# A long convolution and a gated FFN on one core: two filter spectra summed by accumulating transfers, one signal transform split by four, and a new instruction order

## The chip, the cores and the metric

The kernel runs on 1 core of one Trainium2 chip. The metric is device time in microseconds (us) of one execution. The profile comes from one execution, recorded by the hardware profiler.

## What is computed

With S = 2048 positions, D = 640 channels and F = 1728 hidden columns, all in bfloat16:

```
k_shift[t] = sum over u = 0..3 of k[t-u] * shift_k[:, u]
kv  = k_shift * v
y   = causal convolution of kv with ssm_k (length 2048) + kv * ssm_D
h   = x + layernorm(x) * y                 # x is A_q
out = h + (silu(n @ w_gate) * (n @ w_up)) @ w_down,   n = layernorm(h)
```

The reference writes the convolution as an FFT of length 4096. B_x is not used.

## The kernel before

**Blocks.** The sequence is cut into four blocks of 512 positions, i = 0..3, with 128 partitions and four positions to a partition. The filter is cut in the same way, m = 0..3. A block of 512 is taken to 256 complex frequencies by matmuls with a cosine and sine table (`ftab`). A spectrum is a tile of 128 partitions x [4 groups of frequencies][real, imaginary][640], 10,240 bytes on a partition. The output of block i needs the products of the signal spectrum X of block j with the filter spectrum C of block i-j, for all j up to i.

**Transforms.** `halves` (L573) does one in eight PSUM tiles, each of four matmuls of 320 columns (L582): the sums over even and over odd positions, for two groups of frequencies, cosine and sine. ACT evicts each tile (L595). `bfly` (L550, the add at L552) then makes the four groups out of the even and odd halves: four DVE adds or subtractions of 1280 elements for a spectrum. A second way, `quarters` (L613) with `spread` (L635), is in the source and is used by no block: eight tiles of two matmuls each, one position in four to a tile, and eight DVE operations of 1280 elements, of which six come ahead of the first product. A list, `R4` at L463, chooses between them.

**Filter spectra.** The filter is transformed in `kfwd` (L598). C0 and the raw spectra of pieces 1, 2 and 3 are made; R1 is the raw one of piece 1. `kcomb` (L660) then sums neighbours: C1 = R1 + C0, C3 = C3 + C2, C2 = C2 + R1, each as two DVE adds of 2560 elements (L666). C3 has to be summed before C2 is overwritten. For pieces listed in `KD` (L463, empty) it would issue an accumulating transfer from POOL's queue instead (L662), one for each spectrum, and the second would wait for the first.

**Products.** `prod(j, i)` (L743) multiplies X of block j with C of piece i-j for two halves of the frequencies: L753 and L754 multiply 2560 elements each, L759 adds twice 1280, and L769 adds the result into Y. The first product that uses C2 is prod(0, 2), the first that uses C3 is prod(0, 3).

**The rest of a block.** `kv` (L671) loads kT by a transposing transfer (L484 is the helper for those), runs the short convolution on PE (L691, L686), and multiplies by v on DVE; for blocks 1 to 3 the result goes back through transposing transfers into kvo, then L724 multiplies. `ln1` (L778) is the first layernorm: statistics on ACT (L791, L794; block 0 on DVE, L784), a power on POOL (L804), and L813 on ACT. `inverse` (L817) is the transform back (L830), from the tiles IE and IO, evicted by L854 and multiplied with x by L857 (block 0: L845), then the second layernorm with the statistics L868 and L870, the power on POOL (L881) and L886 (block 0: L889); four transposing transfers lay the result down as hnT. `ffn` (L896) is the FFN: 130 matmuls of 512 columns (L911, L912) and five more (L922), silu and a copy by ACT (L934, L936), a product on DVE (L938), and 104 matmuls down (L954), with 8 of half height (L966). ACT evicts their sums (L974) and DVE adds the residual (L981; block 3 does both in L984). SP stores the result (L988).

**What shares bytes.** IO lies on the bytes of kT, IE on those of hnT. X of block 1 lies on bytes of transforms of the filter, X of block 2 on those of R1, and X of block 3 on those of X of block 0. FO, the odd half of a signal transform, lies on kvo.

**Order.** Every operation is a task of a graph with its dependencies (`_Graph.add`, L98). `ORDER` (L307) lists the tasks of each engine, PE, ACT, DVE, POOL and SP, by number in the order of issue. `schedule` (L146) follows these lists and gives out the four PSUM units; its costs and due times only settle which unit a tile gets and how many filler matmuls (L249) PE runs in a long gap. `emit` (L230) writes the instructions with their semaphore waits. Each engine issues strictly in order, so an instruction that waits holds up all that stand behind it on its engine. Nearly all transfers are issued by SP (plain loads by the helper at L479).

Of the kernel before, what the change touches and what calls it, by code (L numbers as in the profile page):

```python
# [58 lines left out]
class _Graph:  # L59
# [170 lines left out]
    def emit(self, block):  # L230
# [75 lines left out]

ORDER = {  # L307
    "pe": """
# [6 lines left out]
    """,  # L315
    "act": """
# [12 lines left out]
    """,  # L329
    "dve": """  # L330
# [10 lines left out]
    """,  # L341
    "pool": """
        5 10 6 8 7 9 11 153 197 218 204 200 211 221 207 214 338 423 405 396 414 531 626 608 599 617 734 838 820 829 811
    """,
    "sp": """
# [3 lines left out]
    """,  # L349
}  # L350

# [1 line left out]
def bass_sequential_preLN__ssm_conv_h3__swiglu_ffn__prompt_kernel(  # L353
# [38 lines left out]
    with ExitStack() as es:  # L392
# [67 lines left out]
        epc = sb("epc", o + 544, [4], f32)  # L460
        assert o + 576 <= SBB + 16481 - A0, o + 576

        BN, DIRECT, D8, PT, BN2, ST, R4, PAIR, WARM, ACC, EA, KD, RD, LA, RA = (0,), (), (), (0,), (), (0,), (), True, 24, (), True, (), (), (1, 2, 3), (0, 1, 2)  # L463
        g = _Graph(nc, es)

        def cpe(n, k):
# [601 lines left out]
```

## Time and profile before

| what | value |
|---|---|
| median of 3 runs | 273.35 us (273.2 to 273.37) |
| span of the profiled execution | 269.5 us; the page gives no other time of that execution |
| granted PE clock, mean | 0.998 |
| filter transforms, PE L582 from KT | 128 matmuls, 299 or 300 ns each as shown |
| signal transforms, PE L582 from vt | 128 matmuls |
| DVE adds of filter spectra, L666 | 6, of 1480 to 1484 ns |
| DVE adds of signal transforms, L552 on X | 16, 818 ns each |
| first FFN matmul of blocks 0, 2, 3 | at 54.44, 168.53 and 222.09 us |

Times are in us from the start of the span. A row of a timeline gives the start, the length, the engine and line, the operation, output and inputs, the count, and in brackets the idle time of the engine ahead of it with what ended it. Matmuls are pipelined, so the mean of one, 300 ns, is longer than the step from one to the next. A row of the groups gives count, busy us and mean ns, and the idle time ahead.

### The profile page before, as it was taken

Reading aid. Unit: us, or ns where it says so; the run is one execution under the profiler, and the core shown is the slowest. Engines: PE = TensorE matmul, PEld = TensorE weight load, DVE = VectorE, ACT = ScalarE, POOL = GpSimd, SP = SyncE. Lnnn points to the kernel's source line nnn. Section 1 sums busy time; section 2 is a strip of 40 time slices with the busy share of each in tenths; the row PEclk is TensorE's granted clock in tenths of the full one; section 3 lists DMA queues with packets and bytes.
Section 4 is the critical chain, followed back from the end, with each engine's and each line's share of the span. In section 5 each row is a group of like instructions: output and inputs, shape, how many; then the busy total and the mean of one; then the engine's idle time right before and its main releaser. Section 6 shows DMA issues by size and latency. Waiting matters only on the chain.

```text
span 269.5 us, 4198 instructions
## 1 busy us (share of the span) xinstructions
PE 255.2 (95%) x1643; PEld 144.2 (53%) x1660; DVE 203.8 (76%) x282; ACT 206.9 (77%) x394; POOL 24.1 (9%) x35
## 2 busy tenths in 40 slices
PE   7799797999999999999999997999999999999995
PEld 5576455545444666554446574454446674444663
DVE  2399999899999999999999998999996100042312
ACT  2799999797889999479969997399889963647400
POOL 0000315000030013000200141000200200000000
PEclk9999999999999999999999999999999999999999
DMA  6999909551173608643000336510000050010002
GB/s 124 373 355 369 340 19 124 112 138 73 30 261 122 103 0 103 135 155 100 0 1 16 86 63 119 129 80 1 2 0 0 2 122 0 2 49 0 0 27 99
DMA packets 42501, 25.85 MB, mean 96 GB/s; under 512 B 32241, under 2 KB 41202, under 8 KB 42482
## 3 DMA queue, kind: packets, MB, share of 16 engines
q1 hardware_dynamic: 41824, 25.58, 35.7%
q8 instruction: 13, 0.21, 0.3%
q10 hardware_dynamic: 658, 0.01, 0.1%
q14 instruction: 6, 0.05, 0.1%
HBM read 15.69 MB, written 2.62 MB: 68 GB/s over the span
## 4 chain that ended last, share of the span: by engine, by line
DVE 41%; PE 27%; ACT 19%; DMA 6%; SPq 3%; issue 2%; POOL 1%; DVEq 0%
PE ps L954 11%; DVE T L753 6%; DVE T L754 6%; PE ps L912 6%; PE ps L911 5%; DVE T L759 5%; DVE Y L769 5%; DVE gu L938 4%; DVE X L552 3%; SPq L484 3%; DMA kT<-in_A_k_dram 3%; ACT KT L543 3%; ACT KO L595 2%; DVE C L666 2%; DMA kc<-in_A_ssm_k_dram 2%
## 5 line engine op out<-in xcount | busy, mean ns | idle before, releaser
L954 PE MATMUL ps<-Wd,gu 128*128 128x384 bf16 (+1 forms) x416 | 59.0, 299 | 0.2 <-ACT qo L854 0.2
L912 PE MATMUL ps<-hnT,UA 128*128 128x512 bf16 x140 | 53.1, 379 | 0.5
L911 PE MATMUL ps<-hnT,GA 128*128 128x512 bf16 x132 | 50.0, 379 | 1.3 <-DMA hnT<-qo 1.3
L954 PEld LDWEIGHTS ps<-Wd,gu 128*128 128x128 bf16 x416 | 40.0, 98 | 18.3 <-issue 1.3
L936 ACT ACTIVATE ub<-ps 128x512 bf16<-128x512 f32 (+1 forms) x60 | 33.7, 568 | 18.5 <-PE ps L912 11.3
L912 PE MATMUL ps<-hnT,UB 128*128 128x512 bf16 x120 | 45.5, 379 | 0.2
L911 PE MATMUL ps<-hnT,GB 128*128 128x512 bf16 x117 | 44.3, 379 | 0.0
L938 DVE TENSOR_TENSOR gu<-gu,ub 128x512 bf16<-128x512 bf16 x52 | 21.5, 421 | 25.1 <-ACT ub L936 13.2
L934 ACT ACTIVATE gu<-ps 128x512 bf16<-128x512 f32 x52 | 29.8, 596 | 12.6 <-PE ps L912 12.4
L753 DVE TENSOR_TENSOR T<-X,C 128x2560 bf16<-128x2560 bf16 x20 | 29.7, 1486 | 0.2
L754 DVE TENSOR_TENSOR T<-X,C 128x2560 bf16<-128x2560 bf16 x20 | 29.7, 1486 | 0.1
L911 PEld LDWEIGHTS ps<-hnT,GA 128*128 128x128 bf16 x140 | 13.7, 98 | 18.2 <-DMA hnT<-qo 1.9
L582 PE MATMUL ps<-KT,ftab 128*128 128x320 bf16 x128 | 19.9, 300 | 2.5 <-ACT KT L543 1.8
L912 PEld LDWEIGHTS ps<-hnT,UA 128*128 128x128 bf16 x140 | 13.7, 98 | 15.7
L881 POOL TENSOR_TENSOR mv<-mv,half 128x1 f32<-128x1 f32 x16 | 13.7, 859 | 68.2 <-ACT mv L874 68.2
L911 PEld LDWEIGHTS ps<-hnT,GB 128*128 128x128 bf16 x120 | 11.7, 98 | 14.2 <-ACT ub L936 0.2
L759 DVE TENSOR_TENSOR T<-T 128x1280 bf16<-128x1280 bf16 x24 | 19.2, 819 | 0.1
L912 PEld LDWEIGHTS ps<-hnT,UB 128*128 128x128 bf16 x120 | 11.7, 98 | 14.0
L582 PE MATMUL ps<-vt,ftab 128*128 128x320 bf16 x128 | 19.0, 299 | 0.1
L804 POOL TENSOR_TENSOR st<-st,half 128x8 f32<-128x8 f32 x4 | 7.9, 1981 | 113.1 <-ACT st L798 113.1
L769 DVE TENSOR_TENSOR Y<-Y,T 128x2560 bf16<-128x2560 bf16 x12 | 17.8, 1484 | 0.0
L582 PEld LDWEIGHTS ps<-KT,ftab 128*128 128x128 bf16 x128 | 11.0, 98 | 10.7 <-ACT KT L543 3.1
(86 smaller groups left out, 376.5 us busy)
## 6 DMA issues: line engine op xcount, KB each, us to landing
kc<-in_A_ssm_k_dram SPq DMA_DIRECT2D x4, 640.0 KB, 10.1
vt<-in_A_v_dram SPq DMA_DIRECT2D x4, 640.0 KB, 4.8
xh<-in_A_q_dram SPq DMA_DIRECT2D x4, 640.0 KB, 5.9
out_dram<-xh SPq DMA_DIRECT2D x16, 160.0 KB, 2.0
Wd<-in_B_w_down_dram SPq DMA_DIRECT2D x1, 1280.0 KB, 7.5
UA<-in_B_w_up_dram SPq DMA_DIRECT2D x1, 1120.0 KB, 13.5
GA<-in_B_w_gate_dram SPq DMA_DIRECT2D x1, 1120.0 KB, 10.5
UB<-in_B_w_up_dram SPq DMA_DIRECT2D x1, 960.0 KB, 7.5
```

What stands on the lines that cost most here:

```text
L582: last = e.matmul(pt.f(c, W), ftab[:, cs, j, f * P:(f + 1) * P], src[:, j, c * W:(c + 1) * W], start=(j == par), stop=(j == par + 2))
L753: g.add("dve", nm, lambda e, x=x, k=k, t1=t1: e.tensor_tensor(out=t1, in0=x, in1=k, op=ALU.mult), cdve(2560), r=[x, k], w=[t1])
L754: g.add("dve", nm, lambda e, x=x, k=ksw, t2=t2: e.tensor_tensor(out=t2, in0=x, in1=k, op=ALU.mult), cdve(2560), r=[x, k], w=[t2])
L759: g.add("dve", nm, lambda e, p=p, q=q, d=d, op=op: e.tensor_tensor(out=d, in0=p, in1=q, op=op), cdve(1280), r=[p, q], w=[d])
L769: g.add("dve", nm, lambda e, y=y, z=z: e.tensor_tensor(out=y, in0=y, in1=z, op=ALU.add), cdve(2560), r=[y, z], w=[y])
L881: g.add("pool", nm, lambda e, m=m: e.tensor_tensor(out=m[:, 3:4], in0=m[:, 2:3], in1=half[:, 1, 0:1], op=ALU.pow), 650, r=[m[:, 2:3], half ...
L911: e.matmul(pt.f(0, N), wg[:, c, f0:f0 + P], hnT[:, c, :], start=(c == 0), stop=(c == NC5 - 1))
L912: last = e.matmul(pt.f(1, N), wu[:, c, f0:f0 + P], hnT[:, c, :], start=(c == 0), stop=(c == NC5 - 1))
L934: g.add("act", nm, lambda e, pt=pt, gv=gv, a=ps_g, ts=ts: e.activation(out=gv, in_=pt.f(a[0], N, a[1])[:, ts], func=ACTF.Silu, scale=gain) ...
L936: g.add("act", nm, lambda e, pt=pt, uv=uv, a=ps_u, ts=ts: e.activation(out=uv, in_=pt.f(a[0], N, a[1])[:, ts], func=ACTF.Copy, scale=gain) ...
L938: g.add("dve", nm, lambda e, uv=uv, gv=gv: e.tensor_tensor(out=gv, in0=gv, in1=uv, op=ALU.mult), cdve(n), r=[gv, uv], w=[gv])
L954: last = e.matmul(pt.flat(c1 - c0, P + c0), slots[fb][:, j * P:(j + 1) * P], Wd[:, fb, c0:c1], start=(fb == 0 and not second), stop=(fb == ...
```

## The change

Three things change. `R4` names `xf2`, so the signal transform of block 2 goes through `quarters` and `spread`. `KD` names 2 and 3, so the sums for C3 and C2 are two accumulating transfers on POOL's queue (L662) and their four DVE adds go; C1 is summed by DVE still. And the lists of `ORDER` are all new.

```
-        BN, ..., R4, PAIR, WARM, ACC, EA, KD, RD, LA, RA = (0,), (), (), (0,), (), (0,), (), True, 24, (), True, (), (), (1, 2, 3), (0, 1, 2)
+        BN, ..., R4, PAIR, WARM, ACC, EA, KD, RD, LA, RA = (0,), (), (), (0,), (), (0,), ('xf2',), True, 24, (), True, (2, 3), (), (1, 2, 3), (0, 1, 2)

 "sp", its beginning, by what the numbers stand for:
-  ident, kT0, kc0, v0, ftab, x0, itab, kc1, UA, PK, kc3, kc2, x1, v1, Wd, UB, PK, GA, Wd, kT1
+  kc0, ident, kT0, x0, ftab, v0, kc2, PK, kc1, kc3, UA, GB, GA, itab, x1, v1, Wd, kT1, PK, Wd, UB
 "sp", the transposing transfers of block 1's hnT and block 2's kvo:
-  hnT, kvo, kvo, hnT, hnT, hnT, kvo, out, kvo, kvo
+  kvo, v2, kvo, kvo, kvo, hnT, kvo, hnT, out, hnT, hnT
 "pool":
-  ... L881 x4 (block 0), L804 (block 1), L881 x4 (block 1) ...
+  ... L881 x4 (block 0), C3 += C2, L804 (block 1), C2 += R1, L881 x4 (block 1) ...
 "pe", ahead of the FFN of block 0:
-  inverse of block 0 as IE, IO, IO, IE
+  inverse of block 0 as IO, IO, IE, IE
 "pe", around the FFN of block 1:
-  30 FFN matmuls, 32 of block 2's transform, 100 FFN matmuls
+  12 of block 2's transform, 10 FFN matmuls, 4 of the transform, 100 FFN matmuls, the five of L922, 20 FFN matmuls
```

In the new order DVE runs the butterflies of C2 and C3 together, ahead of the products of block 0's FFN, and in the new order the first product with C2 stands ahead of the L857 products of block 1, which were partly ahead of it. The inverse of block 1 is also split in another way over the matmuls down of block 0.

More of the change, by code (lines that the diff above doesn't have):

```diff
@@ L308 @@
     "pe": """
[6 rows of a table removed]
[7 rows of a table added]
     """,
     "act": """
[12 rows of a table removed]
[12 rows of a table added]
     """,
     "dve": """
[10 rows of a table removed]
[10 rows of a table added]
     """,
     "pool": """
-        5 10 6 8 7 9 11 153 197 218 204 200 211 221 207 214 338 423 405 396 414 531 626 608 599 617 734 838 820 829 811
+        5 6 10 11 8 7 9 151 202 195 209 205 216 198 212 219 134 336 135 421 403 394 412 529 610 628 601 619 736 822 813 840
+        831
     """,
     "sp": """
[3 rows of a table removed]
[3 rows of a table added]
     """,
@@ L461, in bass_sequential_preLN__ssm_conv_h3__swiglu_ffn__prompt_kernel @@
         assert o + 576 <= SBB + 16481 - A0, o + 576
-        BN, DIRECT, D8, PT, BN2, ST, R4, PAIR, WARM, ACC, EA, KD, RD, LA, RA = (0,), (), (), (0,), (), (0,), (), True, 24, (), True, (), (), (1, 2, 3), (0, 1, 2)
+        BN, DIRECT, D8, PT, BN2, ST, R4, PAIR, WARM, ACC, EA, KD, RD, LA, RA = (0,), (), (), (0,), (), (0,), ('xf2',), True, 24, (), True, (2, 3), (), (1, 2, 3), (0, 1, 2)
         g = _Graph(nc, es)
```

63 rows, old and new, of the table ORDER are left out of this document.

## The prediction

> **What bounds the kernel now.** I read the page's busy times, the table of windows, the chain of waits, and then timelines of PE, DVE, SP and POOL around each place that the diff moves.
>
> ```profile
> span 269.5 us, 4198 instructions
> PE 255.2 (95%) x1643; PEld 144.2 (53%) x1660; DVE 203.8 (76%) x282; ACT 206.9 (77%) x394; POOL 24.1 (9%) x35
> DVE 41%; PE 27%; ACT 19%; DMA 6%; SPq 3%; issue 2%; POOL 1%; DVEq 0%
> ...
> 13.00:54.40 41.40, 36.47 (x311) 23.55 (x313) 39.43 (x60) 39.38 (x65) 6.53 (x9) 1.00 0.80 220
> 54.40:110.00 55.60, 55.34 (x344) 30.71 (x347) 54.65 (x71) 49.24 (x99) 5.72 (x5) 1.00 0.44 105
> 110.00:168.00 58.00, 56.14 (x345) 30.41 (x347) 56.68 (x74) 50.17 (x101) 7.21 (x5) 1.00 0.30 74
> 168.00:222.00 54.00, 53.11 (x308) 29.56 (x313) 38.83 (x53) 44.93 (x94) 3.98 (x5) 1.00 0.16 42
> ```
>
> The windows rows give, after the stretch and its length, busy time and count of PE, weight loads, DVE, ACT, POOL, then granted clock, DMA share and GB/s. I cut them at the first FFN matmul of each block. From 54.4 to 168 us two engines are full side by side: PE (55.3 of 55.6, 56.1 of 58.0) and DVE (54.7 and 56.7). Before 54.4 PE has holes while DVE and ACT are full. So time can come only from the stage ahead of 54.4, from work taken off both PE and DVE, or from PE's few waits.
>
> **The start.** The order of loads changes: SP now issues kc0 first, then ident, kT, xh, ftab, vt; before it was ident, kT, kc0, vt, ftab, xh.
>
> ```profile
> 0.72 0.35 SPq L479 DMA_DIRECT2D ident<-cst_id  x1
> 1.14 3.46 SPq L484 DMA_TRANSPOSE kT<-in_A_k_dram  x1
> 4.66 0.56 SPq L479 DMA_DIRECT2D kc<-in_A_ssm_k_dram  x1
> 6.67 1.92 PE L691 MATMUL ps<-kT,dg 64*64 64x512 bf16 x32 [0.53 <-DMA kT<-in_A_k_dram]
> 9.55 0.75 PE L538 MATMUL ps<-ident,kc 128*128 128x128 bf16 x10 [0.95 <-DMA kc<-in_A_ssm_k_dram]
> 13.03 2.89 PE L582 MATMUL ps<-KT,ftab 128*128 128x320 bf16 x20 [0.36 <-DVE KT L547]
> 13.78 1.30 ACT L595 ACTIVATE C<-ps 128x640 bf16<-128x640 f32 x2 [0.48 <-PE ps L582]
> ```
>
> Before, kc0 stands behind the 3.46 us issue of kT; PE transposes it at 9.55, the first filter transform runs at 13.03, and ACT, from 13.78 on nearly without a hole, evicts its results. Moved ahead of kT, kc0 is issued 3.9 us earlier (4.66 - 0.72, where SP begins). kT is then issued about 0.9 us later, behind kc0 (0.56) and ident (0.35), and PE needs it first too: in the new order the convolution of block 0 (L691, L686) stands whole ahead of the first filter transform, 1.9 us of PE for the 32 of L691. xh ahead of ftab costs one 640 KB transfer and vt behind it gives one back: nothing. I take -1.6 us for the first eviction, between -0.5 (only PE's wait at 9.55 goes) and -2.5.
>
> The next hole is PE's wait for block 1's kT:
>
> ```profile
> 40.42 1.25 PE L830 MATMUL ps<-IE,itab 128*128 128x320 bf16 x8
> 40.61 2.78 SPq L484 DMA_TRANSPOSE kT<-in_A_k_dram  x1
> 47.67 1.06 PE L691 MATMUL ps<-kT,dg 64*64 64x512 bf16 x16 [2.01 <-DMA kT<-in_A_k_dram]
> 51.72 2.88 PE L582 MATMUL ps<-KT,ftab 128*128 128x320 bf16 x20
> 54.44 0.38 PE L911 MATMUL ps<-hnT,GA 128*128 128x512 bf16 x1
> ```
>
> kT shares its bytes with IO, so its load waits until the inverse of block 0 has read IO. Before, PE did IE, IO, IO, IE and the load went out at 40.61, when IO was done; after, PE does both IO tiles first and DVE writes IO ahead of IE, so the load goes out one IE tile earlier (8 matmuls, 1.1 us) beside the shift of the start, and four transforms instead of three stand between. I count the wait as gone, -2.0; bounds 0 (another wait takes its place: ACT's eviction of the last transforms, 39.4 busy of 41.4 us, is the next in line) and -3.1 (2.0 + 1.1). What is late next is ACT. First FFN matmul then: 54.4 - 1.6 - 2.0 = 50.8.
>
> **Block 2's transform split by four.** 32 matmuls become 16, two to a tile in place of four; the eight evictions by ACT stay. On DVE four adds of 1280 elements become eight (L552 before; the helper that the new path uses works on the same shape).
>
> ```profile
> L552 DVE TENSOR_TENSOR X<-X,FO 128x1280 bf16<-128x1280 bf16 x16 | 13.0, 818 | 0.1
> 121.52 2.41 DVE L552 TENSOR_TENSOR X<-X,FO 128x1280 bf16<-128x1280 bf16 x3
> 123.85 1.48 DVE L753 TENSOR_TENSOR T<-X,C 128x2560 bf16<-128x2560 bf16 x1
> ```
>
> A matmul of 320 columns takes not 300 ns of PE but, pipelined, (54.44 - 51.72) / 20 = 0.136 us. PE saves 16 x 0.136 = 2.2 us in a stretch where it is full. DVE issues these adds every (123.85 - 121.52) / 3 = 0.78 us: four more cost 3.1 us. Six of them must precede block 2's first product (two before); the queue is full, so this displaces work and makes no hole by itself.
>
> **Filter sums by transfers.** Four DVE adds of 2560 elements go, and two accumulating transfers of 128 x 10,240 bytes (1280 KB) on POOL's queue come in.
>
> ```profile
> 86.43 1.48 DVE L666 TENSOR_TENSOR C<-C,C 128x2560 bf16<-128x2560 bf16 x1
> 88.36 1.48 DVE L666 TENSOR_TENSOR C<-C,R 128x2560 bf16<-128x2560 bf16 x1
> 93.27 1.48 DVE L666 TENSOR_TENSOR C<-C,C 128x2560 bf16<-128x2560 bf16 x1
> 94.88 1.48 DVE L666 TENSOR_TENSOR C<-C,R 128x2560 bf16<-128x2560 bf16 x1
> 96.80 1.48 DVE L753 TENSOR_TENSOR T<-X,C 128x2560 bf16<-128x2560 bf16 x1
> L857 DVE TENSOR_TENSOR xh<-xh,qo 128x640 bf16<-128x640 bf16 x12 | 5.9, 488 | 4.4 <-ACT qo L854 4.3
> L889 DVE TENSOR_SCALAR qo<-xh,mv 128x640 bf16<-128x640 bf16 x4 | 1.8, 444 | 0.5 <-POOL mv L881 0.4
> 77.25 2.28 POOL L804 TENSOR_TENSOR st<-st,half 128x8 f32<-128x8 f32 x1 [30.01 <-ACT st L798]
> ```
>
> DVE loses 4 x 1.48 = 5.9 us, all between 86 and 96. The sum over DVE is -5.9 + 3.1 = -2.8 us; with the start (-1.6) that makes 4.4, and its holes in the windows above (1.0 us from 54.4 to 110, 1.3 in the next) cover the rest, so it keeps up with a PE that is five us earlier.
>
> The price is a wait. The first transfer (C3 += C2) needs all eight butterflies of C2 and C3, which the new order draws together on DVE ahead of the FFN of block 0: in that order ACT's last three evictions stand just ahead of its first for the FFN, so I put their end 3 us behind the first FFN matmul, at 54. The second (C2 += R1) must not start before the first has landed, and stands on POOL behind the power of block 1's layernorm, which ran at 77.25, that is 22.8 after the first FFN matmul: so it is issued near 50.8 + 22.8 + 2.3 = 76. The first product with C2, at 96.80 before, comes at about 96.8 - 3.6 - 5.9 - 1.5 (three L857 of 0.49 that now stand behind it) = 86. So a landing time of up to 10 us costs nothing; above that DVE stands, and behind it the L857 products of block 1, so the layernorm, hnT and the FFN of block 1: almost one for one.
>
> No accumulating transfer is in this trace. The nearest rows:
>
> ```profile
> Wd<-in_B_w_down_dram SPq DMA_DIRECT2D x1, 1280.0 KB, 7.5
> UA<-in_B_w_up_dram SPq DMA_DIRECT2D x1, 1120.0 KB, 13.5
> GB<-in_B_w_gate_dram SPq DMA_DIRECT2D x1, 960.0 KB, 5.2
> ```
>
> The same bytes as a plain load took 7.5 us on a quiet chip; at GB's rate it would be 6.9; at UA's, among other loads, 15.4, and twice that (31) if reading the destination too doubles it. I take 9, near the Wd row, as few loads run then (DMA share 0.44 on average), and keep 6.9 and 31. So: hidden. Issuing the two costs POOL nothing that is missed, its next step being the L881 of block 1, behind the L857 products.
>
> By the Trainium skill, "DMA: Bandwidth & Descriptors", Anatomy of one DMA, 1280 KB would take 2.0 us plus bytes at 436 GB/s, an estimate of 5.0; the Wd row is slower, and the sum stays as it is. The same page, Rules for kernel authors, says that an accumulate reads its destination and writes it later; no run here shows its price, and it speaks for the long end.
>
> **New order of SP around block 1.** Four of five kvo transposes now stand ahead of the first hnT transposes of block 1, and the fifth behind one:
>
> ```profile
> 100.29 1.20 SPq L484 DMA_TRANSPOSE hnT<-qo  x1
> 101.53 2.58 SPq L484 DMA_TRANSPOSE kvo<-kT  x2
> 168.53 0.39 PE L911 MATMUL ps<-hnT,GA 128*128 128x512 bf16 x1 [1.33 <-DMA hnT<-qo]
> ```
>
> Each holds SP 1.2 to 1.3 us. The convolution matmuls feeding them are moved earlier, so most pass while hnT isn't ready. But PE arrives at the FFN of block 1 earlier, after only 12 matmuls of block 2's transform, and there was no slack before. I add +0.8 for a wait there, between 0 and 1.6 (the 1.33 that block 2 shows, or one transpose more). The waits of block 2 itself I leave as they are.
>
> **Sum.** Start -1.6, kT -2.0, transform -2.2, hnT +0.8, sums 0: -5.0 us. The span of 269.5 becomes 264.5. The page has the span of the profiled execution and no time of its own; the median of the timed runs, 273.35, lies 3.85 above it, and I keep that: **268.3 us**.
>
> **Rivals.**
> 1. *The start doesn't move.* ACT is the wall ahead of 54.4 (39.4 of 41.4), and its evictions are the same in number. Then only the transform counts: about 273.35 - 2.2 = 271.2, between 270 and 272.8. For it: ACT's row. Against it: kc0's place behind kT. 0.14.
> 2. *The transfers land a little late*, at 11 to 15 us: the stall is 1 to 5, the time 269.3 to 273. 0.12.
> 3. *The other side: the second transfer lands late by more than the gain.* Place: the first product with the summed C2. It decides from 10 + 5 = 15 us of landing time for each transfer; at 18 the time is about 276, at 31 (where the second also waits for the first: 55 + 31 + 31 = 117 against 86) about 299. For it: UA's 13.5 us and the destination being read as well. Against it: Wd's 7.5. By the Trainium skill, "SBUF — State Buffer", Who interferes with whom, VectorE in its two-port modes can starve the descriptors that GpSimd writes; here only the four L889 (444 ns each) come near, so it would add less than 2 us. 0.16.
> 4. *The order's own new waits*: with every queue full, hnT late by three or four of the transposes ahead of it at blocks 1 and 2 (2 x 3 x 1.25 = 7.5 against 5.0 and the 0.8 counted): 274 to 276. 0.12.
> 5. *No effect within 0.2%* (0.5 us, about what a measurement of this kernel can tell from no change): 0.04. That the change doesn't do what it says: the listing of the new order has the two transfers, 16 transform matmuls and eight adds, so only their effect is open.
>
> **How the numbers follow.** Forecast, 266 to 270: 0.42. Faster: 0.42 + 0.14 + 0.12 = 0.68; same 0.04; slower 0.16 + 0.12 = 0.28. Range: 265.5 (start -2.5, kT -3.1, no new wait: -7.8) to 276 (rival 4, and rival 3 up to 18 us); most of rival 3 is left out, 0.13, and a little below.
>
> **What would show it.** First eviction near 12.2 and first FFN matmul near 51 (start); no wait of PE for kT; 16 matmuls of the transform and eight adds for block 2, DVE's total near 201; two DMA rows on POOL's queue landing in 7 to 10 us, and DVE's first product with the summed C2 waiting for none of them, at about 86. The prediction fails if that product waits for the transfer, if PE waits longer for hnT at block 1 or 2, or if the first FFN matmul stands at 54 still.

## The result, and the profile after

The kernel after took **269.78 us** (median of 4 runs, 269.68 to 270.21), the kernel before 273.27 us (its three executions above and one more, 272.43 to 273.37): a ratio of 0.9885, 95% interval 0.9853 to 0.9918. The forecast was 268.3, in a range of 265.5 to 276.

The profiled execution of after took 269.68 us, 1.9 us more than its span. From the page, the busy time of each engine and the shares of the chain that ended last:

```profile
span 267.8 us, 4162 instructions
...
PE 254.6 (95%) x1635; PEld 140.1 (52%) x1635; DVE 201.7 (75%) x282; ACT 206.8 (77%) x394; POOL 28.7 (11%) x37
...
PE 41%; ACT 32%; DVE 15%; DMA 5%; SPq 2%; issue 2%; POOL 1%; ACTq 0%; DVEq 0%
```

DVE held 41% of the chain before and holds 15% now; PE went from 27 to 41% and ACT from 19 to 32%. The engine that was relieved holds much less of the chain, and the two others more. The windows, cut at the same times as before (stretch, length, busy time and count of PE, weight loads, DVE, ACT, POOL, then clock, DMA share, GB/s):

```profile
13.00:54.40 41.40, 38.53 (x319) 22.77 (x317) 40.03 (x58) 40.82 (x67) 6.80 (x9) 1.00 0.84 240
54.40:110.00 55.60, 54.40 (x342) 29.91 (x340) 52.60 (x71) 48.81 (x98) 10.32 (x7) 1.00 0.65 139
110.00:168.00 58.00, 56.22 (x345) 29.96 (x344) 57.43 (x76) 50.32 (x101) 6.92 (x5) 1.00 0.30 76
```

Ahead of 54.4 PE, DVE and ACT are all busier (PE 36.5 to 38.5 of 41.4): that is the gain. From 54.4 to 110 PE and DVE are both *less* busy than before (55.3 to 54.4, 54.7 to 52.6): new holes. Lines of after are two higher than those of before (L582 is L584, L911 is L913). PE's milestones, from its timeline (a few matmul records are missing, so a row can be that of the second matmul):

```profile
12.05 1.80 PE L584 MATMUL ps<-KT,ftab 128*128 128x320 bf16 x12 [0.90 <-DMA ftab<-cst_ftab]
...
52.11 0.38 PE L913 MATMUL ps<-hnT,GA 128*128 128x512 bf16 x1
...
112.54 0.38 PE L913 MATMUL ps<-hnT,GA 128*128 128x512 bf16 x1 [0.49 <-ACT FO L628]
...
219.91 0.39 PE L913 MATMUL ps<-hnT,GA 128*128 128x512 bf16 x1 [0.68 <-DMA hnT<-qo]
```

| PE reaches | before | after | shift |
|---|---|---|---|
| first filter transform | 13.03 | 12.05 | -1.0 |
| FFN of block 0 | 54.44 | 52.11 | -2.3 |
| FFN of block 1, with what is left of block 2's transform | 110.21 + 4.35 | 112.54 + 0.54 | -1.5 |
| FFN of block 3 | 221.87 | 219.91 | -2.0 |
| end of the span | 269.5 | 267.8 | -1.7 |

The 222.09 us given for block 3 before are the start of its second matmul (L912); the first, which has no record, stands one step of 0.22 us ahead of it. The third line is the one to look at: with 2.2 us of matmuls less it should have been -4.5, and is -1.5. **Three microseconds are lost at the border of blocks 0 and 1.**

The span fell by 1.7 us, the medians by 3.5. Only a later run explains that: the kernel before has executions with a mean granted clock of 1.00 and others, some 2 us longer, with 0.992 to 0.994, and its profile shows one of the former.

### The profile page after: what moved, and what is told of

Same layout as the page of the kernel before. It is cut to its first block, busy times and chain, and to the rows that moved or that the text cites. A ratio compares the mean times of both kernels' runs of the same rounds, so it can differ in the third digit from the quotient of the medians.

```text
span 267.8 us, 4162 instructions
## 1 busy us (share of the span) xinstructions
PE 254.6 (95%) x1635; PEld 140.1 (52%) x1635; DVE 201.7 (75%) x282; ACT 206.8 (77%) x394; POOL 28.7 (11%) x37
## 4 chain that ended last, share of the span: by engine, by line
PE 41%; ACT 32%; DVE 15%; DMA 5%; SPq 2%; issue 2%; POOL 1%; ACTq 0%; DVEq 0%
PE ps L913 13%; PE ps L914 13%; PE ps L956 8%; PE ps L584 5%; ACT xh L815 4%; ACT ub L938 3%; ACT qo L856 3%; DMA vt<-in_A_v_dram 3%; DVE T L755 3%; ACT qo L872 3%; ACT qo L870 2%; DVE T L761 2%; ACT KT L545 2%; ACT gu L936 2%; DVE gu L940 2%; ACT qo L888 2%
## 5 line engine op out<-in xcount | busy, mean ns | idle before, releaser
L913 PE MATMUL ps<-hnT,GA 128*128 128x512 bf16 x140 | 53.1, 379 | 1.2 <-DMA hnT<-qo 0.7
L913 PE MATMUL ps<-hnT,GB 128*128 128x512 bf16 x120 | 45.5, 379 | 0.7 <-ACT gu L936 0.7
L936 ACT ACTIVATE gu<-ps 128x512 bf16<-128x512 f32 x52 | 30.6, 598 | 17.8 <-PE ps L914 17.6
L938 ACT ACTIVATE ub<-ps 128x512 bf16<-128x512 f32 (+1 forms) x60 | 33.1, 566 | 6.6 <-PE ps L914 3.4
L940 DVE TENSOR_TENSOR gu<-gu,ub 128x512 bf16<-128x512 bf16 x52 | 21.0, 419 | 22.2 <-ACT ub L938 19.6
L913 PEld LDWEIGHTS ps<-hnT,GA 128*128 128x128 bf16 x140 | 13.7, 98 | 18.1 <-DMA hnT<-qo 1.0
L883 POOL TENSOR_TENSOR mv<-mv,half 128x1 f32<-128x1 f32 x16 | 15.3, 965 | 70.7 <-ACT mv L876 70.7
L584 PE MATMUL ps<-KT,ftab 128*128 128x320 bf16 x128 | 20.5, 301 | 2.0 <-DMA ftab<-cst_ftab 0.9
L913 PEld LDWEIGHTS ps<-hnT,GB 128*128 128x128 bf16 x120 | 11.7, 98 | 15.5 <-ACT gu L936 1.7
L806 POOL TENSOR_TENSOR st<-st,half 128x8 f32<-128x8 f32 x4 | 9.1, 2267 | 91.2 <-ACT st L800 91.2
L584 PEld LDWEIGHTS ps<-KT,ftab 128*128 128x128 bf16 x128 | 10.3, 97 | 10.7 <-DMA ftab<-cst_ftab 1.4
L815 ACT ACTIVATE xh<-xh,st 128x640 bf16<-128x640 bf16 x16 | 14.5, 933 | 1.6 <-DVE st L808 1.6
## 6 DMA issues: line engine op xcount, KB each, us to landing
C<-C POOLq DMA_DIRECT2D x1, 1280.0 KB, 13.6
```

Source lines behind the costliest of these rows:

```text
L584: last = e.matmul(pt.f(c, W), ftab[:, cs, j, f * P:(f + 1) * P], src[:, j, c * W:(c + 1) * W], start=(j == par), stop=(j == par + 2))
L815: g.add("act", nm, lambda e, j=j, xj=xj: e.activation(out=xj, in_=xj, func=ACTF.Identity, scale=s[:, 4, j:j + 1], bias=s[:, 5, j:j + 1]), ...
L913: e.matmul(pt.f(0, N), wg[:, c, f0:f0 + P], hnT[:, c, :], start=(c == 0), stop=(c == NC5 - 1))
L936: g.add("act", nm, lambda e, pt=pt, gv=gv, a=ps_g, ts=ts: e.activation(out=gv, in_=pt.f(a[0], N, a[1])[:, ts], func=ACTF.Silu, scale=gain) ...
L938: g.add("act", nm, lambda e, pt=pt, uv=uv, a=ps_u, ts=ts: e.activation(out=uv, in_=pt.f(a[0], N, a[1])[:, ts], func=ACTF.Copy, scale=gain) ...
L940: g.add("dve", nm, lambda e, uv=uv, gv=gv: e.tensor_tensor(out=gv, in0=gv, in1=uv, op=ALU.mult), cdve(n), r=[gv, uv], w=[gv])
```

## The experiments

My theory (A): the start gains 2.3 us; the border gives 3.0 back, because ACT stands there for POOL's power with an eviction behind it that PE needs, and because tiles of two matmuls go at the pace of their evictions; and DVE, once PE is earlier, has no room for the four adds. The rivals: (B) DVE alone is the limit and only the adds' leaving counts; (C) the two transfers cost something at the border; (D) the start is given back in full. Times are medians; each has its ratio to the kernel before on the same chip.

| kernel | us | ratio to before, 95% |
|---|---|---|
| after, a second time | 269.85 | 0.9924 (0.9892 to 0.9956) |
| after, adds back on DVE | 274.74 | 1.0092 (1.0061 to 1.0123) |
| after, transform by halves | 269.09 | 0.9883 (0.9836 to 0.9930) |
| after, old start | 274.17 | 1.0093 (1.0060 to 1.0126) |
| after, border reordered | 267.85 | 0.9852 (0.9797 to 0.9907) |
| after, pieces of 640 B | 269.96 | 0.9954 (0.9939 to 0.9969) |
| after, pieces of 320 B | 274.24 | 1.0103 (1.0081 to 1.0124) |
| before + start | 273.10 | 1.0078 (1.0057 to 1.0099) |
| before + start + transfers | 273.07 | 1.0080 (1.0057 to 1.0103) |
| before + split | 274.37 | 1.0109 (1.0092 to 1.0126) |
| border reordered + halves | 268.57 | 0.9899 (0.9877 to 0.9921) |
| border reordered further | 269.82 | 0.9935 (0.9913 to 0.9958) |

On the three chips of these runs the kernel before took 272.14, 271.48 and 271.41 us (medians), so kernels that ran on different chips are compared to no better than 0.7 us.

### After again

No edit.

> The kernel after, unchanged, beside many runs of the kernel before, each with its span and granted clock. Theory A (the change takes 1.7 us of the span, as the two traces show; the rest of the 3.5 us between the medians comes from runs of before whose granted clock is 0.992 to 0.994 instead of 1.00, in which PE ran at half clock for some 3.4 us): runs of after lie at 269.6 to 270.2 with a clock of 0.998 or more, those of before in two groups, 271 to 272.4 and 273.5 to 274, and the groups of full clock differ by 1.5 to 2.2 us. Rival (time outside the span shrank, or the chips differ): the difference between runs of full clock is 3 us or more.

Ten runs of after: 268.4 to 270.5, all with a clock of 0.998 or more. Fifteen of before: thirteen at 270.3 to 271.6 with 0.998 or more (median 271.3), two at 273.7 and 273.8 with 0.994. At equal clock the change is worth **1.5 us**, near the 1.7 of the spans. The rival, 3 us or more, falls. The time beyond the span was 1.8 to 2.1 us in these runs of both kernels, so it hadn't shrunk. The clocks of the first three runs of before (273.2 to 273.37) are not on record; that they were of the longer kind fits their times and isn't shown.

### The adds back on DVE

```diff
-        ..., True, 24, (), True, (2, 3), (), (1, 2, 3), (0, 1, 2)
+        ..., True, 24, (), True, (), (), (1, 2, 3), (0, 1, 2)
 "dve":
+  C3 += C2 (two adds), C2 += R1 (two adds)      just ahead of the first product with C2
 "pool":
-  C3 += C2, C2 += R1
```

> The kernel after, with the filter sums as eight adds on DVE again (four more than the kernel after, 4 x 1.48 us, just ahead of the first product with the summed C2) and without the two accumulating transfers; start and order of all else as after. Theory A (the adds' leaving matters because DVE is full once PE is earlier): the time goes up by 2 to 5.9 us against the kernel after, to 272 to 275.7, and PE's wait for hnT of block 1 grows. Rival (the adds stood beside a slack DVE, as the prediction's sum of 0 for them has it, and the transfers' traffic costs something at the border of blocks 0 and 1): within 0.7 us of 269.8, or below it.

274.74: 4.9 us more than after. From its timelines, DVE first, then ACT, then PE:

```profile
87.43 2.88 DVE L668 TENSOR_TENSOR C<-C,C 128x2560 bf16<-128x2560 bf16 x2
90.23 2.88 DVE L668 TENSOR_TENSOR C<-C,R 128x2560 bf16<-128x2560 bf16 x2
93.15 1.49 DVE L755 TENSOR_TENSOR T<-X,C 128x2560 bf16<-128x2560 bf16 x1
95.41 0.74 ACT L870 ACTIVATE qo<-xh 128x640 bf16<-128x640 bf16 x1 [5.63 <-DVE xh L859]
95.03 1.19 PE L956 MATMUL ps<-Wd,gu 128*128 128x384 bf16 x6 [2.08 <-DVE gu L940]
98.65 3.63 PE L693 MATMUL ps<-kT,dg 64*64 64x512 bf16 x32 [2.42 <-ACT qo L856]
```

The adds run from 87.43 to 93.11, where after begins its product at 87.47. Behind them on DVE stand L940 (one of the last products of block 0's FFN) and L859: PE stands 2.08 us for the first, ACT 5.63 us for the second. Then a second cost comes on top, in the windows:

```profile
92.00:95.00 3.00, 0.95 (x8) 0.47 (x5) 2.96 (x4) 0.00 (x0) 0.00 (x0) 1.00 0.40 90
95.00:98.00 3.00, 1.19 (x6) 0.51 (x6) 2.93 (x5) 2.56 (x7) 0.00 (x0) 0.61 0.00 0
98.00:101.00 3.00, 2.35 (x24) 1.11 (x28) 2.92 (x5) 2.95 (x7) 0.00 (x0) 0.50 0.00 0
101.00:104.00 3.00, 3.00 (x23) 1.01 (x16) 2.97 (x5) 2.47 (x5) 0.21 (x1) 0.75 0.22 44
92.28:95.69 3.41, 1.33 (x10) 0.77 (x9) 3.38 (x5) 0.28 (x1) 0.00 (x0) 1.00 0.25 55
```

With PE busy for 2.1 of the 6 us from 92 to 98 the granted clock halves, and stays at half past 101 (worked out from the means of the rows, from about 95.7 to 102.5): the 32 matmuls of L693 take 3.63 us instead of 1.93. All ten runs of this kernel show a mean clock of 0.985 to 0.988. By the Trainium skill, "TensorE: Matmul & The Clock Gate", What's actually happening, an idle window of about 3.4 us halves PE's clock and as long a busy one restores it; this trace agrees in the length, about 7 us at half being two such windows, but PE wasn't idle throughout the one ahead of the halving: it was busy for 1.33 of the 3.41 us up to 95.69 (last row).

So A holds: in the new order the adds are on the path at this place on DVE, almost one for one (4.9 us for 5.7 of adds, the clock's share included). The rival, transfers whose leaving brings something, falls; POOL's powers are stretched here too, without any transfer (three in 3.42 us).

### Block 2's transform by halves

```diff
-        ..., (0,), ('xf2',), True, ...
+        ..., (0,), (), True, ...        # the eight tiles and what is left of the adds in the same places of the lists
```

> The kernel after, with block 2's transform by halves again in the same places of the order (PE 16 matmuls more, +2.2 us; DVE -3.1 us of butterflies). Theory A (the quarters' matmuls stand at the border of blocks 0 and 1 and in other work where PE sets the time, but the transform's tiles were seen to be paced by ACT's evictions there): +0.3 to +2.2 us against the kernel after, 270.1 to 272. Rival (DVE is the limit now, and the quarters' butterflies cost more than PE saves): -1 to -3 us, 266.8 to 268.8.

269.09, against 269.78 and 269.85 for after. By ratio no difference can be told. So A's "+0.3 to +2.2" is a miss, and the rival's "-1 to -3" too, narrowly: with 16 matmuls more on PE and four adds less on DVE the time is the same, or 0.7 us lower. Its first matmul of block 1's FFN runs at 112.92, with the whole tiles just ahead of it:

```profile
109.65 3.43 PE L584 MATMUL ps<-vt,ftab 128*128 128x320 bf16 x24
112.92 0.38 PE L913 MATMUL ps<-hnT,GA 128*128 128x512 bf16 x1
```

24 matmuls take from 109.65 to 112.92; in after the 12 in their place take from 109.49 to 112.54. What bounds after here is the last of block 1's four hnT transfers. The rows are, by SP's timeline, the landing time of that transfer (issue to landing), then the third eviction of the tiles on ACT, and the first weight load of the FFN:

```profile
109.81 1.28 SPq L486 DMA_TRANSPOSE hnT<-qo  x1
DMA to landing us min/median/max: 2.6/2.6/2.6
111.43 0.71 ACT L628 ACTIVATE FO<-ps 128x640 bf16<-128x640 f32 x1
112.51 0.10 PEld L913 LDWEIGHTS ps<-hnT,GA 128*128 128x128 bf16 x1 [0.80 <-ACT FO L628]
```

The bracket names the eviction, but that ended at 112.14, and hnT landed at about 112.4, just ahead of the load. So the FFN of block 1 waited for hnT at its end; the evictions had paced the tiles up to 0.3 us before that. The 12 more matmuls of the halves fill that wait, and cost PE 0.4 us there instead of 1.6.

### The split alone

```diff
 kernel before:
-        ..., (0,), (), True, ...
+        ..., (0,), ('xf2',), True, ...        # the tiles and the eight adds in the places of the old ones
```

> The kernel before with block 2's transform by quarters in the places that it had there (16 matmuls of 0.136 us less on PE, 3.1 us of butterflies more on DVE), and nothing else of the change. The prediction's step (PE sets the time there, DVE has room): 2.2 us below before's runs of full clock (271.5), so 269.3. Theory A now (DVE is full, and a tile of two instead of four matmuls is paced by its eviction): between -0.7 and +2 us against 271.5.

274.37: 3 us **slower** than before, beyond even A's range. PE's timeline at the transform (before, the 32 matmuls began at 116.68 and the next FFN matmul on record at 121.39):

```profile
116.72 0.72 PE L622 MATMUL ps<-vt,ftab 128*128 128x320 bf16 x4
117.69 1.04 PE L622 MATMUL ps<-vt,ftab 128*128 128x320 bf16 x4 [0.25 <-ACT ub L938]
...
119.47 0.44 PE L622 MATMUL ps<-vt,ftab 128*128 128x320 bf16 x2 [0.15 <-ACT X L628]
120.07 0.45 PE L622 MATMUL ps<-vt,ftab 128*128 128x320 bf16 x2 [0.15 <-ACT X L628]
...
121.49 0.38 PE L914 MATMUL ps<-hnT,UA 128*128 128x512 bf16 x1 [0.38 <-ACT FO L628]
...
136.54 0.39 PE L913 MATMUL ps<-hnT,GB 128*128 128x512 bf16 x1 [1.55 <-ACT gu L936]
132.00 0.60 ACT L938 ACTIVATE ub<-ps 128x512 bf16<-128x512 f32 x1 [3.21 <-DVE gu L940]
```

Half the matmuls take the same time, 4.77 us against 4.71. Tiles start 0.60 us apart, because ACT evicts one in that time (four in 2.49 us), and the two matmuls of a tile need 0.27. PE saves nothing. What is left is the butterflies' 3.1 us on DVE: at 136.54 PE waits 1.55 us for ACT, and ACT has waited 3.21 us at 132.00 (last row) for a product that stands behind them on DVE.

### The old start under the new order

```diff
 every list:
-  order of after up to the FFN of block 0
+  order of before up to the FFN of block 0, then after's
```

> The kernel after, with the order of before on every engine and queue up to the FFN of block 0, and after's order behind it. Theory A (what the start gained, 2.3 us at the first FFN matmul, is carried to the end): first FFN matmul back near 54.4, time +1.8 to +2.5 us, 271.6 to 272.3. Rival (the border of blocks 0 and 1 waits for something that does not depend on the start, so the start's gain is given back there): within 0.7 us of 269.8.

274.17, 4.4 us more (4.2 by its six executions with a clock of 0.998 or more, median 273.98), well above what A allowed. The first FFN matmul runs at 52.90, not at 54.4. DVE's timeline has the rest:

```profile
58.40 0.42 DVE L726 TENSOR_TENSOR vt<-vt,kvo 128x512 bf16<-128x512 bf16 x1 [2.80 <-DMA kvo<-kT]
58.75 1.48 DVE L756 TENSOR_TENSOR T<-X,C 128x2560 bf16<-128x2560 bf16 x1
60.15 3.88 DVE L554 TENSOR_TENSOR C<-C,KO 128x1280 bf16<-128x1280 bf16 x5
63.95 1.28 DVE L726 TENSOR_TENSOR vt<-vt,kvo 128x512 bf16<-128x512 bf16 x2
```

Five butterflies of the filter stand between DVE's products for block 1's signal, which PE wants at 61.5 and gets at 65.2. In after the five ran from 55.42 to 59.2, ahead of all these products, and PE began this transform at 60.90. So the edit moved not only the start but also them, and the 4.4 us are not the start's alone.

### The new start alone, and with the transfers

```diff
 kernel before, every list:
-  order of before up to the FFN of block 0
+  order of after up to the FFN of block 0, then before's
 and, in the second kernel:
-        ..., True, (), (), ...
+        ..., True, (2, 3), (), ...     # both transfers on POOL around block 1's first power, four adds less, butterflies of C2, C3 pulled up
```

> The kernel before with after's order up to the FFN of block 0 on every engine and queue, and nothing else of the change: eight adds on DVE, halves for block 2. Theory A (the start's gain needs no other part): first FFN matmul at 52 to 52.5, time 2 to 2.5 us below before's runs of full clock, 269.2 to 269.8. Rival B (DVE is full between the start and block 1, so that without the transfers an earlier PE only waits longer, for hnT of block 1 or for products of DVE): within 0.8 us of before, 271 to 272.5.

> The kernel before with after's start and its two accumulating transfers (four adds less), but block 2's transform by halves and before's order at the border of blocks 0 and 1. Theory A (the border cost 3 us through the new order there, above all an eviction behind ACT's wait for POOL): 1 to 2 us faster than the same parts in the order of after, which took 269.09: 267 to 268. Rival (whatever is won in front of the border is lost there again, because DVE and ACT are full with it): 269 to 270.

273.10 and 273.07, both 1.6 us *slower* than before (1.8 at equal clock); both theories missed both. The first weights of the FFN are loaded at 52.0 and 52.3, so the gain arrives. It is lost at once, as ACT's and DVE's timelines of the first kernel show:

```profile
55.43 3.76 DVE L554 TENSOR_TENSOR C<-C,KO 128x1280 bf16<-128x1280 bf16 x5
59.22 1.63 DVE L726 TENSOR_TENSOR vt<-vt,kvo 128x512 bf16<-128x512 bf16 x3
60.77 1.48 DVE L756 TENSOR_TENSOR T<-X,C 128x2560 bf16<-128x2560 bf16 x1
62.17 0.42 DVE L940 TENSOR_TENSOR gu<-gu,ub 128x512 bf16<-128x512 bf16 x1
62.62 0.60 ACT L938 ACTIVATE ub<-ps 128x512 bf16<-128x512 f32 x1 [4.35 <-DVE gu L940]
```

The FFN's product L940 stands behind 6.7 us of other DVE work; ACT waits 4.35 us for its buffer, and PE for ACT. In after the same butterflies and three products of L726 stand ahead of L940 (at 60.76), and ACT, which has statistics of block 1 to do in that time, waits 0.54 us for it. So the order of ACT's queue decides too. And the four adds that the second kernel saves bring nothing: behind the start, in before's order, they are not on the path. Together with the run that put them back into after: whether work on DVE is hidden depends on the order round it.

### The border reordered

On ACT the third convolution eviction (L717) and the last group's statistics go ahead of the square root that waits for POOL; two smaller moves go with it.

```diff
 "act":
-  L870 L872 (third), L886 (waits for POOL), L876, L717 (third), L976, L888, L886 L886, L870 (last), L888, L872 (last)
+  L870 L872 (third), L717 (third), L870 L872 (last), L886 (waits for POOL), L876, L976, L888, L886 L886, L888
 "dve":  L859 of the last group right behind that of the second
 "sp":
-  hnT, kvo (fifth), hnT
+  kvo (fifth), hnT, hnT
```

> The kernel after, with the order at the border of blocks 0 and 1 changed: on ACT the third eviction of the convolution and the two statistics of the third row group stand ahead of the square root that waits for POOL's power, on DVE the product of the third row group stands earlier, on SP the fifth transpose of kvo stands ahead of the first of hnT. Theory A (3 us were lost there because ACT stood for POOL with that eviction behind it, and kvo came late behind hnT): the FFN of block 1 starts 1 to 2 us earlier than 112.54 and the time falls by 1 to 2 us, to 267.8 to 268.8. Rival (the four evictions of the split tiles on ACT and the last hnT pace the border whatever stands ahead): within 0.5 us of 269.8.

267.85, 1.9 us less than after. In after, POOL, ACT and PE at this place:

```profile
97.47 4.69 POOL L883 TENSOR_TENSOR mv<-mv,half 128x1 f32<-128x1 f32 x3 [21.02 <-ACT mv L876]
100.85 0.29 ACT L886 ACTIVATE mv<-mv 128x1 f32<-128x1 f32 x1 [1.79 <-POOL mv L883]
101.24 0.57 ACT L717 ACTIVATE kT<-ps 128x512 bf16<-128x512 f32 x1
101.87 0.45 PE L968 MATMUL ps<-Wd,gz 64*128 64x384 bf16 x4 [1.09 <-ACT kT L717]
```

and here:

```profile
98.85 0.57 ACT L717 ACTIVATE kT<-ps 128x512 bf16<-128x512 f32 x1
101.00 0.28 ACT L886 ACTIVATE mv<-mv 128x1 f32<-128x1 f32 x1
111.71 0.38 PE L913 MATMUL ps<-hnT,GA 128*128 128x512 bf16 x1
```

ACT uses the time in which it stood; the eviction ends 2.4 us earlier and PE's wait is gone. The last hnT transfer goes out at 108.71 instead of 109.81, and the FFN of block 1 starts 0.8 us earlier (1 to 2 expected), and block 3's at 217.7 against 219.9, so the rest comes from later waits that shrank. One of its four runs took 269.57, and the interval overlaps that of after: the wait that went is shown, the 1.9 us of the whole are not clear of the noise.

### The border with halves, and reordered further

```diff
 on top of the border reordered, first kernel: block 2's transform by halves
 second kernel, "act": L876, L886 and L888 of the last group earlier (ahead of two L976)
 second kernel, "sp":  the store of the output between the hnT transposes goes behind the last
```

> The kernel after with the border's order of the run that took 267.85 (the third eviction of the convolution and the third row group's statistics ahead of ACT's wait for POOL, the fifth transpose of kvo ahead of the first of hnT), and block 2's transform by halves again. Theory A (split and order are separate: halves cost nothing or win 0.7 us, as they did in after's own order): 267.0 to 267.9. Rival (with the border's waits gone PE sets the time there, and the 16 matmuls more count): 269 to 270.

> The same border order as in the run that took 267.85, by quarters, and two steps more: ACT's add of epsilon for the third row group, its square root and its scaling stand earlier (POOL's last power of block 1 then runs near 102 instead of 106), and on SP a store of the output stands behind the last two transposes of hnT. Theory A (the FFN of block 1 waits at 111.7 for the last hnT, which waits for that power): it starts 0.5 to 0.9 us earlier, and the time is 267.0 to 267.4. Rival (the tiles of block 2's transform, paced by their evictions on ACT, end no earlier): within 0.3 us of 267.85.

268.57 and 269.82, on another chip than the run before. The first lies between both expectations. The second is a miss for A and not near the rival's figure either, but its mechanism is the rival's: POOL's four powers end at 103.05 and hnT is issued by 109.37, earlier than ever, and lands 2.6 us behind its issue of 108.09, at 110.7. PE at the FFN of block 1 now does wait for an eviction (the row is the second matmul; the first weights are loaded at 111.65):

```profile
111.88 0.38 PE L914 MATMUL ps<-hnT,UA 128*128 128x512 bf16 x1 [0.38 <-ACT FO L628]
```

So the tiles of two matmuls pace the border once the rest is out of the way. This FFN starts no earlier than in the reordered border (111.63 there, by the weights), and later PE waits 0.50 us for ACT at 127.98 and 0.71 for hnT of block 3 at 219.06, which it didn't there. Why these waits are back is open. Neither kernel beats the reordered border.

### Slower transfers

```diff
-e.dma_start(dst[:], prev[:], accum_op=ALU.add, max_dma_last_dim=2560)
+e.dma_start(dst[:], prev[:], accum_op=ALU.add, max_dma_last_dim=640)     # second kernel: 320
```

> The kernel after with the two accumulating transfers cut into pieces a quarter as long (640 B instead of 2560 B), nothing else. Theory A (the second transfer has 3 us to spare, as the first product with the summed C2 ran at 87.47 without a wait and the transfer landed near 84.5; beyond that each us of landing costs about one): if it lands in under 12 us the time stays within 0.5 us of 269.8; if in 15 us, about 272; if in 20 us, about 277, and that product shows a wait for a DMA. Rival (a late product only moves work on DVE that has slack): within 0.7 us of 269.8 however late it lands.

> The kernel after with the pieces of the two accumulating transfers an eighth as long (320 B instead of 2560 B). At 640 B the second landed 11.1 us after its issue at 75.2 and nothing waited. Theory A (3 us to spare, then one for one): if both take 15 to 18 us, the second lands at 90 to 95, DVE's product with the summed C2 stands 3 to 8 us, and the time is 272.5 to 278. Rival (a late product shifts work within DVE's slack): within 0.7 us of 269.9.

Issue to landing, last column, in after, then at 640 B, then at 320 B:

```profile
C<-C POOLq DMA_DIRECT2D x1, 1280.0 KB, 13.6
C<-R POOLq DMA_DIRECT2D x1, 1280.0 KB, 9.4
```

```profile
C<-C POOLq DMA_DIRECT2D x1, 1280.0 KB, 14.0
C<-R POOLq DMA_DIRECT2D x1, 1280.0 KB, 11.1
```

```profile
C<-C POOLq DMA_DIRECT2D x1, 1280.0 KB, 16.0
C<-R POOLq DMA_DIRECT2D x1, 1280.0 KB, 16.4
```

269.96 and 274.24. At 11.1 us nothing waits. At 16.4 the first product with C2 does:

```profile
92.27 1.49 DVE L755 TENSOR_TENSOR T<-X,C 128x2560 bf16<-128x2560 bf16 x1 [4.71 <-DMA C<-R]
```

4.71 us of wait there, 4.4 us in the time. A holds, and the rival of slack on DVE falls. Part of it is the clock again (0.987 to 0.993), as PE stands for DVE.

## Why the prediction was right in sign and too large in size

**The start (-1.6 and kT -2.0; measured -2.3: -1.0 at the first transform, -1.3 behind it).** The mechanism came as described: kc0 early, first eviction at 12.80 (12.2 forecast, 13.78 before), and kT's load at 38.29 instead of 40.61, so PE's 2.01 us for it are gone. But three waits took their places: 0.84 us for ident and 0.90 for ftab, both behind kc0 on SP, and 1.01 for ACT before the convolution. The bound "another wait takes its place: ACT" was the right one. First FFN matmul at 52.11, not 50.8.

**Transform by quarters (-2.2; measured nothing on PE where it stands alone).** This is the step that failed. "PE saves 16 x 0.136 = 2.2 us in a stretch where it is full" counted matmuls and said that the eight evictions "stay". They stay, and they set the pace: 0.60 us for a tile whose two matmuls need 0.27. The split alone took as long on PE as the halves and cost 3 us through DVE; in after's order halves are as good.

**hnT at block 1 (+0.8; measured +3.0 at that border).** A wait for hnT was expected at the right place, and it came (one of the prediction's own signs of failing): without any wait the twelve tile matmuls would have ended at 109.49 + 12 x 0.136 = 111.1, and hnT landed at 112.4. That is 1.3 us, within the 0 to 1.6 allowed. The evictions' pace lies inside the same stretch (the twelve matmuls and the wait take 3.05 us instead of 1.63) and would have cost most of it without hnT, so the two can't be told apart there. What the sum left out is the 1.09 us of the eviction behind ACT's wait for POOL, shown by moving it; the remaining 0.5 I did not trace. Rival 4, the order's own new waits, was thus partly true, and cost 3 us, not 7.5.

**Filter sums (0; right for the transfers, not for the adds in the new order).** The first transfer was issued at 59.49 (54 forecast), the second at 75.14 (76 forecast) and landed in 9.4 us (9); the product ran at 87.47 (86) with no wait, DVE's total is 201.7 (201). The first took 13.6 us, beyond the 7 to 10, without a cost. So "hidden", said of the transfers, held. The 0 for the adds' leaving holds only where they are off the path: put back into the new order just ahead of the first product with C2, they cost 4.9 us, part of it half a clock. The prediction's own sum over DVE, in which their leaving lets it keep up with an earlier PE, pointed that way. Rival 3's place was right, and its slope too: 4.4 us at 16.4. Its tie at 15 was a little late: the wait begins at about 12 (75.14 + 12.3 = 87.47), and a tie lies where the wait reaches the gain, by the 1.5 to 1.7 us of the whole change at 13.5 to 14.

**Not counted:** blocks 2 and 3. Up to the FFN of block 3 another 0.5 us is gained (before's waits of 0.61 and 1.33 us at 162.86 and 168.53 are gone, others of 0.55 and 0.68 have come at 128.90 and 219.91), and 0.3 is lost behind it, which I did not trace. In the span, with the transform counted by its matmuls and its pace within the 3.0: -2.3 - 2.2 + 3.0 - 0.5 + 0.3 = -1.7.

**The 3.85 us beyond the span.** I carried the distance from the span to the median over to after. It was not a constant: about 1.9 us of it lie outside the span, the rest was most likely that the profiled execution had the full clock and the three timed ones had not. Sign and size by medians (-3.5) look nearer to the forecast (-5.0) than the change itself is (-1.5 to -1.7). That 268.3 lies only 1.5 us from 269.78 is in part luck: the forecast span, 264.5, was 3.3 us too short, and the distance added to it 1.9 too long.

**Still open:** what each part is worth in the whole. The start and the split added to before singly gave +1.8 and +3.0 at equal clock, all parts together in their order -1.5; the two edits of the start each moved filter butterflies too, and the transfers alone in before's order were not tried.

## What to carry to other kernels

Price a smaller tile on the engine that empties it as well as on the one that fills it: a tile takes the longer of the two. Work on a full engine is hidden or not by what stands behind it in that engine's queue; when the order is new, look up the queue anew instead of carrying the cover over. Where the releaser that a row names ended long before the wait did, look for a transfer that landed later. And before comparing a span with a median, compare their granted clocks.

## What the runs showed of the hardware

- An accumulating transfer of 1280 KB from one tile to another took 9.4 to 13.6 us in pieces of 2560 B, 11.1 to 14.0 at 640 B and 16.0 to 16.4 at 320 B; its issue held POOL for 1.3 to 1.5, 2.1 to 2.3 and 3.2 to 3.4 us.
- POOL's power on 128x1 takes 0.55 us at 107.77, where DVE has a hole, and three of them 4.69 us at 97.47 (the first alone 3.34), beside DVE's additions and products. One at 96.22 in the kernel before took 0.55 us beside DVE's work too, so DVE's work alone doesn't settle the length. By the Trainium skill, "SBUF — State Buffer", Who interferes with whom, a DVE instruction with two inputs in SBUF contends with a GpSimd instruction that reads SBUF; the long rows fit that; the one at 96.22 doesn't show it.
- A PE that was busy 2.1 of 6 us lost half its clock for about 7 us (a mean clock of 0.987 over 271.9 us). It was busy for 1.33 of the 3.41 us ahead of that.
